# Attention and two expert layers on one core: token chunks in reversed order with split openings, and exponentials per stack with a bias and a second result

## The chip, the cores and the metric

The kernel runs on one core of a Trainium2 chip. The metric is the device time of one execution in microseconds (us), the median of several executions. The engines are named as the profile names them: PE is TensorE (matrix products), PEld its weight loads, DVE is VectorE, ACT is ScalarE, POOL is GpSimd, SP is SyncE, whose queue issues the transfers. L846 is line 846 of the kernel before; the changed kernel's numbers are a few higher and are given where they are used.

## The reference

Three stages follow one another, in float32 (w_in and w_out come as float64):

```python
# 2 batches, 8 heads, 576 positions, head width 64; q and k are drawn 8 times larger
scores = q @ k.T / sqrt(64)
mask_plain = (rel >= 0) & (rel < 32)                       # heads 0 to 3
mask_dil   = (rel >= 0) & (rel < 128) & (rel % 4 == 0)     # heads 4 to 7
scores = where(mask, scores, -1e9);  scores -= max(scores)
attn = exp(scores);  attn /= sum(attn) + 1e-9
x = (attn @ v) as 1152 tokens x 512

p = domain_probs / (sum(domain_probs) + 1e-9)              # 4 experts
x = sum over e of p[:, e] * (relu(x @ w1[e]) @ w2[e])      # hidden width 1024 each

h = x @ w_in                                               # hidden width 2048
out = (h - tanh(h)) @ w_out
```

## The kernel before

**Tokens and slices.** The 1152 tokens are cut in two sets: g = 0 holds tokens 0 to 511 (four chunks of 128; a half is 256), g = 1 holds 512 to 1151 (five chunks; a half is 320). The hidden layers are cut in 12 slices of 512 columns: 0 to 7 are the four experts', two each, and 8 to 11 belong to the second layer (w_in, w_out). A hidden slice of a set lies in four tiles f = 0 to 3 of 128 hidden columns, each as a rounded high part and a low rest, and each in two halves of the set's tokens.

The places in the program are counted by n = 0 to 13. At n = 0 and 1 (EARLY) set 0 alone goes through slices 0 and 1, in plain products of 256 columns (`whole`, L742). At n = 2 to 7 both sets go through slices 2 to 7. At n = 8 and 9 set 1 catches up on slices 0 and 1. At n = 10 (N2) to 13 (LAST) both sets go through the second layer.

**Two kinds of step on PE.** An "h" step makes a product: from n = 2 on the hidden layer is made with seven block products instead of eight (Winograd's scheme). ORDER takes products 1, 5, 6, 2, 3, 7, 4, each for t = 0 and 1, so a set has 14 such steps of six matmuls (L803). Products 2 and 3 complete halves 0 and 1 of tile f = t; products 7 and 4 complete half 1 and half 0 of tile f = t + 2. The sums that this needs run on DVE and POOL (L720, L128), then `hidden` follows. For experts that is `relu`: ACT writes the high part (L723), DVE the low one (L726), which is also what frees the PSUM bank. In the second layer it is a tanh (L774), a subtraction on DVE, and for one half a copy on ACT (L790) and a subtraction on DVE (L128).

A "y" step is one chunk of 128 tokens: 12 matmuls of 128x512 (four tiles f, three high/low passes each, L846) that accumulate in one bank. Then DVE adds the bank to the running sum `acc` (L867, L876); a sum's first addition is an ACT copy instead (L865, L871). After the experts `x2_step` transposes `acc` on PE (L892), and the second layer's input is prepared from that.

**What sets the order.** A list `steps` is written out by the rules of L926 to L940: `hs` and `ys` give a set's product and chunk steps, and `merge(a, b, at)` puts the chunks b between the products a at the places `at`. All else (sums, relus, weight splits on ACT L165 and POOL L128, attention for set 1, decoding) is handed to `later` or `when` with a due time on a planned clock that advances by `duration` of each step. `need(key)` makes everything that carries that key be written ahead of the step. Each engine executes its rows in the order written. In the kernel before, a chunk needs `("h", g)`: all pending work of that set's whole hidden slice. The slices n > 2 are merged: chunks of one set lie between the products of the other.

**Attention** has 16 head-chunks, eight for set 0 in the first 35 us (`first_attention`), eight of five stacks for set 1 during the early slices. A head-chunk holds 4 or 5 stacks of 96 keys for 128 queries. Its stages are scores (PE), `largest` (DVE L496 scale and mask, DVE L502 the negated maximum per stack, POOL L503 adds it), `exps` (ACT L510, one instruction over all stacks), `norm` (DVE L515 sums per stack, L516 and L517 add and invert, POOL L519 scales), transposes (PE L529, ACT L536) and values (PE L569).

**Decoding.** w_in and w_out are float64. DVE takes their bits apart (L672, L676, L684, L689, with ACT L683 between), 32 blocks of 128x512. Their due times are spread over a stretch [a, b) of a place n by `a + (b - a) * i / m`.

## Time and profile before

| | |
|---|---|
| median of 3 executions | 698.28 us (696.35 to 699.21) |
| the profiled execution: its time, its span | 698.15 us, 696.4 us |
| mean granted PE clock | 0.97 |
| PE busy | 641.1 us of the span (92%) |
| DVE, POOL, ACT busy | 452.2 us (65%), 381.9 us (55%), 291.7 us (42%) |
| chain of work that ended last | PE 52%, DVE 24%, POOL 8%, issue 7%, DMA 4%, ACT 4% |

Busy shares are means over the whole program. The places where PE waits are single, and few; they are read one by one from its timeline. The granted clock is a share of 2.4 GHz; the other level in this profile is 0.5, 1.2 GHz, so a clock below 1 over a stretch tells how much of the stretch ran at half speed.

### The profile page before, as it was taken

Reading aid. Unit: us, or ns where it says so; the run is one execution under the profiler, and the core shown is the slowest. Engines: PE = TensorE matmul, PEld = TensorE weight load, DVE = VectorE, ACT = ScalarE, POOL = GpSimd, SP = SyncE. Lnnn points to the kernel's source line nnn. Section 1 sums busy time; section 2 is a strip of 40 time slices with the busy share of each in tenths; the row PEclk is TensorE's granted clock in tenths of the full one; section 3 lists DMA queues with packets and bytes.
Section 4 is the critical chain, followed back from the end, with each engine's and each line's share of the span. In section 5 each row is a group of like instructions: output and inputs, shape, how many; then the busy total and the mean of one; then the engine's idle time right before and its main releaser. Section 6 shows DMA issues by size and latency. Waiting matters only on the chain.

```text
span 696.4 us, 10915 instructions
## 1 busy us (share of the span) xinstructions
PE 641.1 (92%) x4095; PEld 553.9 (80%) x4095; DVE 452.2 (65%) x859; ACT 291.7 (42%) x656; POOL 381.9 (55%) x352
## 2 busy tenths in 40 slices
PE   7876999999999999999999897999899968998997
PEld 3575878798888988978888787888698857986995
...
PEclk9998999999999999999999999899999997998999
...
GB/s 322 305 192 58 62 81 102 1 1 107 92 105 107 91 114 143 47 160 98 53 191 60 95 147 1 181 77 98 54 1 71 82 91 106 122 76 76 1 46 91
DMA packets 36693, 68.06 MB, mean 98 GB/s; under 512 B 4128, under 2 KB 10400, under 8 KB 36640
## 3 DMA queue, kind: packets, MB, share of 16 engines
...
## 4 chain that ended last, share of the span: by engine, by line
PE 52%; DVE 24%; POOL 8%; issue 7%; DMA 4%; ACT 4%; SPq 0%; DVEq 0%; POOLq 0%; ACTq 0%
PE bank_f L846 21%; PE bank_f L803 12%; PE bank_s L846 8%; POOL w L128 4%; DVE h L726 3%; PE bank_a L846 3%; PE bank_s L803 3%; DVE single L689 3%; DVE single L676 2%; DVE single L684 2%; DVE single L672 2%; DMA double<-in_moe_w_out_dram 2%; DVE bank_f L720 2%; DMA in<-single 2%; PE bank_a L803 2%
## 5 line engine op out<-in xcount | busy, mean ns | idle before, releaser
L846 PE MATMUL bank_f<-w,h 128*128 128x512 f32 x876 | 223.2, 403 | 16.9 <-ACT h L790 8.0
L846 PEld LDWEIGHTS bank_f<-w,h 128*128 128x128 f32 x876 | 163.6, 193 | 56.4 <-ACT h L790 11.1
L128 POOL TENSOR_TENSOR w<-raw,w 128x512 fp32r<-128x512 f32 x110 | 145.2, 1326 | 108.3 <-ACT w L165 105.1
L803 PE MATMUL bank_f<-x,w 128*128 128x320 f32 (+1 forms) x1218 | 180.2, 300 | 4.4 <-DVE h L726 4.4
L803 PEld LDWEIGHTS bank_f<-x,w 128*128 128x128 f32 x1218 | 172.5, 191 | 10.2 <-DVE h L726 5.4
L720 POOL TENSOR_TENSOR sums<-u,p 128x320 f32<-128x320 f32 (+1 forms) x44 | 39.4, 899 | 97.0 <-DVE u L720 97.0
L846 PE MATMUL bank_s<-w,h 128*128 128x512 f32 x312 | 80.5, 408 | 5.6 <-ACT h L723 4.5
L165 ACT ACTIVATE w<-raw 128x512 fp32r<-128x512 f32 x112 | 68.7, 627 | 30.5 <-POOL raw L128 11.6
L846 PEld LDWEIGHTS bank_s<-w,h 128*128 128x128 f32 x312 | 60.0, 197 | 20.0 <-ACT h L723 5.4
L803 PE MATMUL bank_s<-x,w 128*128 128x320 f32 (+1 forms) x402 | 61.5, 298 | 1.5 <-DVE h L726 1.5
L803 PEld LDWEIGHTS bank_s<-x,w 128*128 128x128 f32 x402 | 57.2, 190 | 4.1 <-DVE h L726 2.2
L128 POOL TENSOR_TENSOR w<-sum,w 128x512 fp32r<-128x512 f32 x36 | 49.4, 1373 | 19.0 <-ACT w L165 19.0
L867 DVE SCALAR_TENSOR_TENSOR acc<-bank_f,pn,acc 128x512 f32<-128x512 f32 x43 | 32.1, 747 | 40.3 <-PE bank_f L846 40.0
L723 ACT ACTIVATE h<-bank_f 128x320 fp32r<-128x320 f32 (+2 forms) x83 | 35.0, 430 | 41.4 <-DVE bank_f L720 40.7
L726 DVE SCALAR_TENSOR_TENSOR h<-bank_f,h 128x320 fp32r<-128x320 f32 (+2 forms) x83 | 38.9, 474 | 13.7 <-ACT h L723 12.7
L683 ACT ACTIVATE double<-double 128x512 f32<-128x512 f32 x32 | 21.6, 676 | 56.7 <-DVE single L676 51.4
L676 DVE SCALAR_TENSOR_TENSOR single<-double,single 128x512 int32<-128x512 int32 x32 | 40.6, 1269 | 1.1
L815 ACT ACTIVATE p<-bank_f 128x320 f32<-128x320 f32 (+1 forms) x60 | 23.5, 418 | 37.7 <-PE bank_f L803 37.7
L165 ACT ACTIVATE w<-sum 128x512 fp32r<-128x512 f32 x36 | 22.7, 630 | 39.3 <-POOL sum L615 21.3
L689 DVE SCALAR_TENSOR_TENSOR single<-double,single 128x512 f32<-128x512 f32 x32 | 33.3, 1042 | 8.6 <-ACT double L683 7.9
L803 PE MATMUL bank_a<-x,w 128*128 128x320 f32 (+1 forms) x228 | 37.0, 298 | 1.0 <-DVE h L726 1.0
L803 PEld LDWEIGHTS bank_a<-x,w 128*128 128x128 f32 x228 | 33.3, 190 | 2.3 <-DVE h L726 1.3
...
## 6 DMA issues: line engine op xcount, KB each, us to landing
...
```

The lines of the kernel that those rows point to most:

```text
L128: engine.tensor_tensor(out=out, in0=a, in1=b, op=ALU.subtract)
L165: nc.scalar.activation(out=hi, in_=src, func=ACTF.Copy)
L676: nc.vector.scalar_tensor_tensor(out=t, in0=high, scalar=-0x40000000, in1=t, op0=ALU.bitwise_and, op1=ALU.bitwise_or)
L683: nc.scalar.activation(out=mag, in_=mag, func=ACTF.Square)
L689: nc.vector.scalar_tensor_tensor(out=w, in0=mag, scalar=HIGH_MIN * HIGH_MIN, in1=w, op0=ALU.is_ge, op1=ALU.mult)
L720: e.tensor_tensor(out=o, in0=x, in1=y, op=ALU.add)
L723: nc.scalar.activation(out=hi, in_=src, func=ACTF.Relu)
L726: nc.vector.scalar_tensor_tensor(out=lo, in0=src, scalar=0.0, in1=hi.bitcast(F32), op0=ALU.max, op1=ALU.subtract)
L803: nc.tensor.matmul(out=b, lhsT=w[:, wi, kk, t * 128:(t + 1) * 128], rhs=x[:, kk, xi, :], start=(kk == 0 and i == 0), stop=(kk == 1 and i = ...
L815: nc.scalar.activation(out=pt[P], in_=b, func=ACTF.Copy)
L846: nc.tensor.matmul(out=y, lhsT=a, rhs=b_, start=(f == 0 and m == 0), stop=(f == NF - 1 and m == 2),)
L867: nc.vector.scalar_tensor_tensor(out=t, in0=y, scalar=p, in1=t, op0=ALU.mult, op1=ALU.add)
```

## The change

Four things change.

1. **Exponentials.** `largest` no longer has POOL add the negated maximum. `exps` issues one ACT instruction per stack of 96 keys (4 or 5 a head-chunk), with the negated maximum as its bias and the sum of its results as a second output. `norm` no longer sums on DVE.
2. **Chunks.** The chunks of a set run from the last tokens to the first (`c = last - i`). What a chunk waits for is told by tile and half instead of by set.
3. **Split openings.** `direct` cuts the first two chunks of a set in "ya" (the first tiles: three at n = 0 and 1, else two) and "yb" (the rest). It is used where the chunks follow their own set's products: n = 0 and 1, n = 2 set 0, n = 8, and n = 10 set 0. From n = 2 on the first "ya" stands ahead of the set's last product.
4. **Due times.** In the second layer the decoding's stretch goes from [a + 8, b) to [a + 4, b - 8). Set 1's attention starts 6 us later with 10.5 instead of 11 us from pair to pair. Some merge places are one earlier.

```diff
+MAKES = {
+    1: lambda t: (), 5: lambda t: (), 6: lambda t: (), 2: lambda t: (t, 0), 3: lambda t: (t, 1),
+    7: lambda t: (t + 2, 1), 4: lambda t: (t + 2, 0),
 }
...
-            nm = st.tile([128, 5], F32, tag="nm", name="nm")
-            s, r, spread = self.by_stack(t[:, 0], nm)
+            nm = self.nm[a] = st.tile([128, 5], F32, tag="nm", name="nm")
+            s, r, _ = self.by_stack(t[:, 0], nm)
             nc.vector.tensor_reduce(out=r, in_=s, axis=AX.X, op=ALU.max, negate=True)
-            later(0.5 * self.lag, lambda: nc.gpsimd.tensor_tensor(
-                out=s, in0=s, in1=spread, op=ALU.add
-            ))
 
         def exps(self, a):
-            n = self.n * BK
-            t = self.t[a]
-            nc.scalar.activation(out=t[:, 1, :n], in_=t[:, 0, :n], func=ACTF.Exp)
+            t, nm = self.t[a], self.nm[a]
+            sm = self.sm[a] = st.tile([128, 5], F32, tag="sm", name="sm")
+            for j in range(self.n):
+                ks = slice(j * BK, (j + 1) * BK)
+                nc.scalar.activation(
+                    out=t[:, 1, ks], in_=t[:, 0, ks], func=ACTF.Exp, bias=nm[:, j:j + 1],
+                    accum_out=sm[:, j:j + 1],
+                )
 
         def norm(self, a):
-            sm = st.tile([128, 5], F32, tag="sm", name="sm")
+            sm = self.sm[a]
             p, r, _ = self.by_stack(self.t[a][:, 1], sm)
-            nc.vector.tensor_reduce(out=r, in_=p, axis=AX.X, op=ALU.add)
             nc.vector.tensor_tensor(out=r, in0=r, in1=eps[:, :self.n], op=ALU.add)
...
-        key = ("h", g)
+        key = ("h", g, f, half)
...
-        later(0.0, lambda: sums_of(n, g, P, t, b, done), ("h", g))
+        later(0.0, lambda: sums_of(n, g, P, t, b, done), ("h", g, *MAKES[P](t)))
...
-            later(0.5, lambda: add(u5, u, p5, nc.gpsimd), ("h", g, t, "u5"))
+            later(0.5, lambda: add(u5, u, p5, nc.gpsimd), ("u5", g, t))
...
-    def y_step(n, g, c):
-
-        need(("h", g), ("w2", n))
-        y, done = f_bank()
-        fs = range(NF)
+    def y_step(kind, n, g, i):
+
+
+
+        c = SETS[g][1] // 128 - 1 - i
+        first = 3 if n < EARLY else 2
+        fs = {"y": range(NF), "ya": range(first), "yb": range(first, NF)}[kind]
+        if n < EARLY:
+            need(*[("h", g, f) for f in fs])
+        else:
+            halves = {c * 128 // QH[g], (c * 128 + 127) // QH[g]}
+            need(*[("h", g, f, half) for f in fs for half in halves])
+        need(("w2", n))
+        y, done = opened.pop((g, c)) if kind == "yb" else f_bank()
+        if kind == "ya":
+            opened[g, c] = y, done
...
-    FIRST, LATE, THEN = (1, 2, 3, 4, 5), (4, 5, 6, 7, 8), (5, 7, 10, 13)
+    def direct(h, n, g):
+
+        cs = ys(n, g)
+        (a0, b0), (a1, b1) = [[(kind, *step[1:]) for kind in ("ya", "yb")] for step in cs[:2]]
+        if n < EARLY:
+            return h + [a0, a1, b0, b1] + cs[2:]
+        return h[:-1] + [a0] + h[-1:] + [a1, b0, b1] + cs[2:]
+
+    FIRST, LATE, THEN = (1, 2, 3, 4, 5), (3, 4, 5, 6, 8), (5, 7, 10, 13)
     steps = []
     for n in range(EARLY):
-        steps += hs(n, 0) + ys(n, 0)
-    steps += hs(EARLY, 0) + ys(EARLY, 0) + hs(EARLY, 1)
+        steps += direct(hs(n, 0), n, 0)
+    steps += direct(hs(EARLY, 0), EARLY, 0) + hs(EARLY, 1)
...
     for n in range(NS1, N2 - 1):
-        steps += hs(n, 1) + ys(n, 1)
-    steps += hs(N2 - 1, 1) + merge(hs(N2, 0), ys(N2 - 1, 1), LATE) + ys(N2, 0) + hs(N2, 1)
+        steps += direct(hs(n, 1), n, 1)
+    steps += hs(N2 - 1, 1) + direct(merge(hs(N2, 0), ys(N2 - 1, 1), LATE), N2, 0) + hs(N2, 1)
     for n in range(N2 + 1, LAST + 1):
-        first = FIRST if n > N2 + 1 else LATE
+        first = (2, 3, 4, 5, 6) if n > N2 + 1 else LATE
...
         if n > N2:
-            a += 8.0
+            a, b = a + 4.0, b - 8.0
...
-    BEAT = 11.0
+    BEAT = 10.5
     for n in range(4):
         pair = Pair(kinds[1, n < 2], n % 2, {"s": "s", "t": "a", "x": "a"})
-        due = 3.0 + BEAT * n
+        due = 9.0 + BEAT * n
...
-        when(BEAT * 3 + 20.0 + 4.0 * c, lambda c=c: prep(1, c, True, nc.vector, nc.gpsimd), ("x", 1, False))
+        when(BEAT * 3 + 25.0 + 3.0 * c, lambda c=c: prep(1, c, True, nc.vector, nc.gpsimd), ("x", 1, False))
```

The change moves instructions as well as adding them. First place: DVE at n = 0, while the four hidden tiles of slice 0 get their low parts (`h0_702` and `h0_750` are tiles 1 and 2, `xf` and `x0` the preparation of set 0's input, `w2` a weight split, `sm` and `att` set 1's attention). Before:

```order
L128 TENSOR_TENSOR w2_703<-raw_603,w2_703 128x512
L128 TENSOR_TENSOR x0_712<-xf_383,x0_712 128x256
L128 TENSOR_TENSOR xf_383<-xf_383 128x256
L726 SCALAR_TENSOR_TENSOR h0_702<-bank_f_645,h0_702 128x512
L128 TENSOR_TENSOR xf_383<-xf_383 128x256
L128 TENSOR_TENSOR x0_751<-xf_383,x0_751 128x256
L515 TENSOR_REDUCE sm_756<-att_686 128x5
L516 TENSOR_TENSOR sm_756<-sm_756,eps_104 128x5
L517 RECIPROCAL sm_756<-sm_756 128x5
L128 TENSOR_TENSOR x0_712<-xf_383,x0_712 128x256
L128 TENSOR_TENSOR xf_383<-xf_383 128x256
L726 SCALAR_TENSOR_TENSOR h0_750<-bank_f_717,h0_750 128x512
```

After, from the same weight split:

```order
L133 TENSOR_TENSOR w2_685<-raw_611,w2_685 128x512
L133 TENSOR_TENSOR x0_689<-xf_390,x0_689 128x256
L133 TENSOR_TENSOR xf_390<-xf_390 128x256
L732 SCALAR_TENSOR_TENSOR h0_684<-bank_f_653,h0_684 128x512
L133 TENSOR_TENSOR xf_390<-xf_390 128x256
L133 TENSOR_TENSOR x0_726<-xf_390,x0_726 128x256
L133 TENSOR_TENSOR x0_689<-xf_390,x0_689 128x256
L133 TENSOR_TENSOR xf_390<-xf_390 128x256
L732 SCALAR_TENSOR_TENSOR h0_725<-bank_f_694,h0_725 128x512
L501 SCALAR_TENSOR_TENSOR att_786<-bank_s_746,mask_1_True_102 128x480
L507 TENSOR_REDUCE nm_788<-att_786 128x5
```

From this split on tile 2's low part (L726, now L732) is no longer behind the attention's sums (L515 to L517). Two scale-and-mask rows with their maxima (L496, L502), which before stand just ahead of this piece, now stand behind it (L501, L507).

Second place: PE at n = 8, where set 1's last products of slice 0 meet its own chunks (`h8_0_1` is tile 0 of set 1; `w2` and `w1` are weights, `x1` operands made from set 1's input). Before:

```order
L803 MATMUL bank_f_4579<-x1_1585,w1_4294 128x320 x6
L803 MATMUL bank_f_4591<-x1_1585,w1_4294 128x320 x6
L846 MATMUL bank_s_4607<-w2_4441,h8_0_1_4515 128x512 x3
L846 MATMUL bank_s_4607<-w2_4462,h8_1_1_4528 128x512 x3
L846 MATMUL bank_s_4607<-w2_4477,h8_2_1_4516 128x512 x3
L846 MATMUL bank_s_4607<-w2_4501,h8_3_1_4529 128x512 x3
L846 MATMUL bank_s_4625<-w2_4441,h8_0_1_4515 128x512 x3
L846 MATMUL bank_s_4625<-w2_4462,h8_1_1_4528 128x512 x3
L846 MATMUL bank_s_4625<-w2_4477,h8_2_1_4516 128x512 x3
```

After:

```order
L810 MATMUL bank_f_4603<-x1_1642,w1_4331 128x320 x6
L866 MATMUL bank_f_4615<-w2_4465,h8_0_1_4539 128x512 x3
L866 MATMUL bank_f_4615<-w2_4486,h8_1_1_4552 128x512 x3
L810 MATMUL bank_s_4625<-x1_1642,w1_4331 128x320 x6
L866 MATMUL bank_s_4636<-w2_4465,h8_0_1_4539 128x512 x3
L866 MATMUL bank_s_4636<-w2_4486,h8_1_1_4552 128x512 x3
L866 MATMUL bank_f_4615<-w2_4501,h8_2_1_4540 128x512 x3
L866 MATMUL bank_f_4615<-w2_4525,h8_3_1_4553 128x512 x3
L866 MATMUL bank_s_4636<-w2_4501,h8_2_1_4540 128x512 x3
L866 MATMUL bank_s_4636<-w2_4525,h8_3_1_4553 128x512 x3
```

The first chunk's tiles 0 and 1 now stand ahead of the last product, and tiles 2 and 3 of the first two chunks behind the openings of both.

Third place: DVE at the end of n = 11, set 1, the sums after products 7 and 4 (`u`, `sums`; `h11_2_1` is tile 2 of set 1), chunk additions (`acc`), and decoding (`single`, `double`). Before:

```order
L720 TENSOR_TENSOR bank_a_5939<-bank_a_5939,u_5781 128x320
L128 TENSOR_TENSOR x0_1440<-bank_s_5929,x0_1440 128x320
L128 TENSOR_TENSOR bank_a_5939<-bank_a_5939,sums_1439 128x320
L672 TENSOR_SCALAR single_5971<-double_5906 128x512
L676 SCALAR_TENSOR_TENSOR single_5971<-double_5906,single_5971 128x512
L876 TENSOR_TENSOR acc_5195<-bank_f_5950,acc_5195 128x512
L684 SCALAR_TENSOR_TENSOR single_5971<-double_5906,single_5971 128x512
L128 TENSOR_TENSOR h11_2_1_5829<-bank_a_5939,h11_2_1_5829 128x320
L720 TENSOR_TENSOR bank_f_5978<-bank_f_5978,u_5815 128x320
L689 SCALAR_TENSOR_TENSOR single_5971<-double_5906,single_5971 128x512
L128 TENSOR_TENSOR bank_f_5978<-bank_f_5978,sums_1439 128x320
L128 TENSOR_TENSOR h11_3_1_5860<-bank_f_5978,h11_3_1_5860 128x320
```

After:

```order
L726 TENSOR_TENSOR bank_a_5970<-bank_a_5970,u_5814 128x320
L133 TENSOR_TENSOR x0_1448<-bank_s_5960,x0_1448 128x320
L133 TENSOR_TENSOR bank_a_5970<-bank_a_5970,sums_1447 128x320
L897 TENSOR_TENSOR acc_5227<-bank_f_5981,acc_5227 128x512
L133 TENSOR_TENSOR h11_2_1_5860<-bank_a_5970,h11_2_1_5860 128x320
L726 TENSOR_TENSOR bank_f_6006<-bank_f_6006,u_5844 128x320
L133 TENSOR_TENSOR bank_f_6006<-bank_f_6006,sums_1447 128x320
L133 TENSOR_TENSOR h11_3_1_5893<-bank_f_6006,h11_3_1_5893 128x320
L897 TENSOR_TENSOR acc_5523<-bank_f_6037,acc_5523 128x512
```

The four decoding rows (L672, L676, L684, L689) that stood between the sums and the hidden tiles 2 and 3 are gone from here; the chunk addition follows the sums directly.

## Rows read from the trace of the kernel before

**Rows 1.** Page, parts 1 and 2: busy times, and PE's granted clock in tenths, 40 slices.

```profile
PE 641.1 (92%) x4095; PEld 553.9 (80%) x4095; DVE 452.2 (65%) x859; ACT 291.7 (42%) x656; POOL 381.9 (55%) x352
...
PEclk9998999999999999999999999899999997998999
```

**Rows 2.** PE's waits: line waited for and releaser: us in total, times, longest.

```profile
PE bank_a L529 <- POOL att L519: 9.1, 2, 8.1
...
PE bank_f L803 <- DVE h L726: 4.4, 4, 1.3
```

**Rows 3.** Five windows: PE, PEld, DVE, ACT, POOL busy (count), PEclk, DMA share, GB/s.

```profile
40.00:60.00 20.00, 11.87 (x114) 11.01 (x114) 18.20 (x34) 8.48 (x19) 11.40 (x15) 0.83 0.29 104
...
390.00:410.00 20.00, 17.69 (x83) 14.39 (x82) 12.81 (x22) 6.72 (x17) 6.21 (x6) 0.91 0.47 171
...
420.00:440.00 20.00, 16.17 (x77) 14.01 (x76) 12.45 (x25) 6.63 (x16) 16.28 (x13) 0.83 0.02 3
...
560.00:580.00 20.00, 11.92 (x57) 9.61 (x56) 15.80 (x28) 8.17 (x19) 10.79 (x10) 0.80 0.29 83
...
620.00:640.00 20.00, 16.97 (x75) 13.75 (x74) 11.78 (x21) 6.68 (x16) 9.42 (x8) 0.83 0.22 72
```

**Rows 4.** PE's timeline: start, us, work [idle before <- releaser].

```profile
57.08 1.09 PE L529 MATMUL bank_a<-ident,att 128*96 128x128 f32 x4 [8.13 <-POOL att L519]
...
122.22 2.23 PE L846 MATMUL bank_f<-w,h 128*128 128x512 f32 x8 [1.10 <-DVE h L726]
...
200.00 1.03 PE L846 MATMUL bank_a<-w,h 128*128 128x512 f32 x3 [0.70 <-ACT h L723]
...
397.76 0.33 PE L892 MATMUL bank_s<-ident,acc 128*128 128x128 f32 x1 [1.91 <-DVE acc L867]
...
432.75 1.65 PE L846 MATMUL bank_s<-w,h 128*128 128x512 f32 x3 [3.83 <-ACT h L723]
...
485.31 0.77 PE L892 MATMUL bank_s<-ident,acc 128*128 128x128 f32 x5 [1.18 <-DVE sums L128]
...
493.82 1.54 PE L846 MATMUL bank_f<-w,h 128*128 128x512 f32 x4 [0.90 <-DVE h L128]
...
571.38 0.73 PE L846 MATMUL bank_f<-w,h 128*128 128x512 f32 x2 [3.35 <-ACT h L790]
...
575.20 0.79 PE L846 MATMUL bank_f<-w,h 128*128 128x512 f32 x1 [3.09 <-DVE h L128]
...
577.63 1.65 PE L846 MATMUL bank_f<-w,h 128*128 128x512 f32 x3 [1.65 <-ACT h L790]
...
631.26 1.65 PE L846 MATMUL bank_f<-w,h 128*128 128x512 f32 x3 [1.44 <-ACT h L790]
```

**Rows 5.** Timelines of DVE and ACT at two of these waits.

```profile
52.69 0.68 DVE L726 SCALAR_TENSOR_TENSOR h<-bank_f,h 128x512 fp32r<-128x512 f32 x1
...
57.23 0.68 DVE L726 SCALAR_TENSOR_TENSOR h<-bank_f,h 128x512 fp32r<-128x512 f32 x1
...
429.15 0.63 ACT L165 ACTIVATE w<-sum 128x512 fp32r<-128x512 f32 x1 [3.74 <-POOL sum L128]
```

**Rows 6.** Lines by form: busy, mean ns | idle before; attention, ACT copies, decoding.

```profile
L510 ACT ACTIVATE att<-att 128x384 f32<-128x384 f32 x8 | 4.1, 517 | 8.7 <-POOL att L503 8.6
...
L503 POOL TENSOR_TENSOR att<-att,nm 128x384 f32<-128x384 f32 x8 | 6.6, 824 | 7.0 <-DVE nm L502 6.9
...
L515 DVE TENSOR_REDUCE sm<-att 128x4 f32<-128x384 f32 x8 | 4.4, 548 | 2.7 <-ACT att L510 2.7
...
L865 ACT ACTIVATE acc<-bank_f,pn 128x512 f32<-128x512 f32 x9 | 6.1, 682 | 7.2 <-PE bank_f L846 7.2
...
L871 ACT ACTIVATE acc<-bank_f 128x512 f32<-128x512 f32 x5 | 2.9, 589 | 3.8 <-PE bank_f L846 3.8
...
L676 DVE SCALAR_TENSOR_TENSOR single<-double,single 128x512 int32<-128x512 int32 x32 | 40.6, 1269 | 1.1
```

**Rows 7.** ACT's timeline, 0 to 8 us: the smallest exponential.

```profile
2.03 0.23 ACT L1139 ACTIVATE first_exp<-zero 128x32 bf16<-128x32 bf16 x1
```

More of the change, by code (lines that the diff above doesn't have):

```diff
@@ L849, in y_step @@
                 )
[L850 removed]
+        if kind != "ya":
+            later(0.0, lambda: y_sum(n, g, c, y, done), ("y", n, g))
     def y_sum(n, g, c, y, done):
```

24 lines of the change are left out of this document (15 added, 9 removed).

## The prediction

> **What bounds the kernel now.** I read the page first: PE is busy for 641.1 of 696.4 us, DVE 65%, POOL 55%, ACT 42% [rows 1]. So PE's own work is the floor, and a change that leaves its matmuls as they are, as this one does, can win only in PE's gaps and in the stretches where its clock stands at half. The row of granted clocks reads 9 in 36 of 40 slices and 8 or 7 in four [rows 1]: the losses sit in few places. I then asked for PE's waits by releaser. The longest single wait, 8.1 us, is for POOL's scaling in the attention; a group of waits of at most 1.3 us for DVE's low part is another kind [rows 2]. Windows around the long waits show a clock of 0.83, 0.91, 0.83, 0.80 and 0.83 over 20 us each [rows 3]. With levels 1 and 0.5, a mean of 0.83 is (1 - 0.83) x 20 / 0.5 = 6.8 us at half speed, 0.91 is 3.6 us, 0.80 is 8 us. PE's timeline then gives each wait its place and releaser [rows 4]; two short timelines tell what the releaser was itself behind [rows 5]. The profiled execution took 698.15 us, 0.13 below the median of 698.28, so the sum against it needs no correction.
>
> **The change part by part.**
>
> *Slice 0 (n = 0).* PE has finished its first products at 48.95 (57.08 less the wait of 8.13) and then stands still until a transpose of set 1's attention is released [rows 4]. Tile 1's low part comes at 52.69 and tile 2's at 57.23 [rows 5]: DVE was late with both. The order shows what goes from ahead of tile 2: two L496 and two L502 rows and one chain L515 to L517. A 128x384 L515 takes 0.55 us [rows 6], these are a quarter wider: some 0.65 us for each of five, and a few tenths for the chain's two small ones, 3.6 us. Tile 2 then comes at about 53.6. PE can open two chunks with tiles 0 to 2, 18 matmuls, before tile 3. At 0.23 us each at full speed (0.43 at half) these are 4 to 8 us of work that before lay behind 57.08. Tile 3 itself is hardly earlier, since the attention's rows now stand ahead of it. I take -5.0. Bounds: 0, if tile 2 is still late for another reason (its weights, POOL), and -9.5, the wait plus 1.4 us of half clock (6.8 us at half, of which 4.0 are idle until 57.08, so 2.8 x 0.5).
>
> *n = 2.* The first own chunk waits 1.10 us for DVE's low part [rows 4]; split and reversed, it begins with a tile finished several products before. -1.0, bounds 0 and -1.1.
>
> *Reversed chunks, slices 3 to 6.* At 200.00 the first chunk of set 1 waits 0.70 us for the relu of the last product [rows 4]; with its like in slices 4 to 6 that makes four. Product 4, the last, makes half 0, and the first chunk now reads half 1, ready two products (1.7 us) earlier: 4 x 0.70 = -2.8, bounds 0 and -2.8.
>
> *Slice 7's transposes.* PE waits 1.91 us for the addition of a chunk that it has only just made [rows 4], because the first transposes stand ahead of the own chunks. Now one whole chunk (12 matmuls, 2.7 us) stands ahead and covers the wait. With the 3.6 us at half behind it [rows 3], worth 1.8, that is -3.7, bounds 0 and -3.7.
>
> *n = 8.* PE waits 3.83 us for a relu [rows 4]. ACT had this relu behind a weight split which itself waited 3.74 us for POOL [rows 5]: the weight chain is late, not the products. The split opening puts 12 matmuls there where four ran before; eight more are 8 x 0.23 = 1.8 us of cover, and about 2 us of wait stay. Of the 3.4 us that 6.8 us at half cost here [rows 3] I take 1.0 back. -2.8, bounds 0 and -7.2.
>
> *n = 10.* Waits of 1.18 and 0.90 us [rows 4]. The split opening covers most of the second, earlier merge places part of the first: -1.5, bounds 0 and -2.1.
>
> *n = 11 to 12.* Three waits, 3.35 + 3.09 + 1.65 = 8.1 us [rows 4]: the last tiles' sums on DVE stand between decoding rows, of which L676 alone takes 1.27 us [rows 6]. The order shows all four decoding rows gone from this place, and a set 0 product more ahead of the first chunk. 8 us at half [rows 3], most of it idle, cost about 1.6 more. I take -7.0, bounds -2 (the waits' third, if the chain of tanh, subtraction and copy is what is late) and -9.7.
>
> *n = 12 to 13.* 1.44 us [rows 4] and 6.8 us at half [rows 3], nearly all busy, which cost 2.7: same cause. -3.5, bounds 0 and -4.1.
>
> *Exponentials.* A head-chunk loses POOL's addition, 0.82 us, and DVE's sum, 0.55 us [rows 6]. ACT did 384 columns in 0.517 us [rows 6] and 32 in 0.23 [rows 7], a slope of 0.82 ns a column, so 96 columns are 0.28 us. ACT copies with a per-partition operand take 0.682 against 0.589 us [rows 6], so a bias may add 0.09: 0.28 to 0.37 us a row, 1.1 to 1.5 for four, +0.6 to +1.0 a head-chunk. No row has a second output on ACT; its bounds are 0 and one more smallest row, 0.23 us. That leaves 1.1 to 2.4 us for four and the chain of one head-chunk between 0.8 us shorter and 0.5 longer. Eight head-chunks follow one another in the first 35 us, over four engines; only what ends the last of them counts in full. I take -1.0 for the whole, bounds -3 and +4 (eight times 0.5). For set 1, five rows in a row hold up ACT's relus by at most 3 us, which the PSUM banks in turn cover; if that cover is gone, it is a wait as at 200.00.
>
> On such rows the Trainium skill, ScalarE: Activation LUTs, section What ACT_TABLE_LOAD costs, states 280 ns + 0.833 ns a column with a pointer as bias, and about 93 ns of overlap from one to the next. By it four rows would take, as an estimate, 4 x 0.36 - 3 x 0.09 = 1.16 us, and the term would be as taken. It has no price for the second output.
>
> What goes on as before: the waits of 1.0 to 1.3 us for the low part of L726 once a slice [rows 2], since decoding in slices 3 to 7 keeps its times.
>
> *Sum:* 5.0 + 1.0 + 2.8 + 3.7 + 2.8 + 1.5 + 7.0 + 3.5 + 1.0 = 28.3, so 698.15 - 28.3 = 669.9: **670 us**.
>
> **The rivals.**
>
> *(a) Other chains end the waits.* POOL, ACT and DVE are late with weights and decoding, and PE's splitting only moves the wait by a few matmuls. For it: the ACT row behind POOL at n = 8 [rows 5]. Decoding that is moved earlier also lands beside POOL's splits; L676 takes 1.27 us on the mean [rows 6], and what slows it slows POOL as well. Then slice 0 gives 2, n = 8 gives 1, n = 11 gives 3, n = 12 gives 1.5, the reversal and the transposes 6.5: 14, so 684 us. Against it: at slice 0 and n = 11 the DVE rows named are in the order, and are gone. (The Trainium skill, SBUF — State Buffer, section SBUF: two separate sides, states that a DVE row with two SBUF inputs and a POOL row that reads SBUF lock each other out. The trace agrees as far as L676, two such inputs, takes 1.27 us on the mean [rows 6] against 0.68 for L726 with one of its inputs in PSUM [rows 5]; it does not show who held it up.)
>
> *(b) All of it is given back*, with the clock: the sum of the far bounds, 9.5 + 1.1 + 2.8 + 3.7 + 7.2 + 2.1 + 9.7 + 4.1 + 3 = 43, so 655 us. For it: each clock drop follows a wait. Against: at n = 8 the weight chain stays.
>
> *(c) Set 1's preparation is late.* Its attention begins 6 us later, its last preparation is due at 59.5 instead of 57, and PE reaches it earlier by what slice 0 gives. By the planned durations (2 x (8 x 1.44 + 4 x 2.73) for n = 0 and 1, 14 x 0.72 + 4 x 2.73 for n = 2) set 1's first product stands at 65.9. The cover of 8.9 falls to 6.4, and by 5 more in truth. A wait of up to 6 us at that product: 676 us. Against: the attention also costs less DVE and POOL.
>
> *(d) Slower: ACT becomes the bound.* If a row with a second output costs 1.3 us or more, ACT, busy 8.48 us of 20 at slice 0 [rows 3], gets 32 x 1.3 - 4.1 = 37 us more in the first 35 and 40 x 1.3 less some 5 = 47 in the next 85. The first attention ends some 20 us later and relus wait behind exponentials for 10 more: that is the point where the gains of 28 are gone, about 700 us or above. Against: the smallest row takes 0.23 us [rows 7], so it would need five times that.
>
> *(e) The change doesn't do what it says*: tiles are waited for as a whole, or in the order of an engine's latest row, so finer keys and splits release nothing, and only decoding and reversal count, 7.0 and 2.8: 688 us. Against: the orders differ at the three places.
>
> **How the numbers follow.** The forecast has 0.50; (a) 0.18; (b) 0.15; (c) 0.08; (d) 0.04; (e) 0.05. The predicted time is the forecast's, 670. 652 to 688 holds the forecast, (a), (c) and most of (b), leaving out (d), half of (e) and a third of (b): about 0.88 by these cases, less with costs that I don't know of. About 0.5%, 3.5 us, is what a measurement of this kernel can tell from no change. Faster by over that 0.92. The other 0.08 are (d) and what of (a) and (e) may come out worse than priced: within it 0.04, slower 0.04.
>
> **What would show it.** Slice 0: PE busy with chunk rows between 50 and 57 us, tile 2's low part near 53.6. Slices 3 to 6: no wait at the first chunk. Transposes: a whole chunk ahead, no wait. n = 8: a wait of about 2 us, ended by ACT behind a weight split. n = 11: at most 1 us in all, and full clock. Exponentials: rows of 0.28 to 0.6 us. PE's busy time should fall by the half clock's 8 or 9 us and its idle time by about 20. It is wrong if exponentials take 1 us, or if long waits stand in the same places behind L165 or a decoding row.

## The result, and the profile after

The changed kernel takes 675.5 us, the median of four executions (674.65 to 680.58), against 698.36 us for the kernel before, measured beside it: a ratio of 0.969 (95% interval 0.965 to 0.974). The forecast was 670 us, the range 652 to 688, the sum of the gains 28.3 us; 22.9 us came.

The profiled execution is the longest of the four: 680.58 us, a span of 678.8. Its mean granted clock is 0.980, against 0.986 to 0.992 in the other three. PE ran at half speed from 27.4 to 37.6 us in it, and the first attention took 36.04 us, against 32.44 to 33.34 in experiments 1, 2, 10, 11 and 12, which have the same code there: about 3 of the 5 us to the median lie in this place. Where the rest lies is not shown, since the other three have no trace. The page's first part and its row of granted clocks, after:

```profile
PE 638.0 (94%) x4095; PEld 554.6 (82%) x4095; DVE 437.8 (65%) x843; ACT 307.0 (45%) x784; POOL 367.3 (54%) x336
...
PEclk9888999999999999999999998979899999999999
```

Against [rows 1] PE is busy 3 us less and the span is 17.6 us shorter, so most of the gain is idle time (14.5 us). The prediction looked for 8 or 9 us less of busy time and about 20 of idle time: both fall short. PE's waits by releaser, after:

```profile
PE bank_f L866 <- ACT h L729: 3.9, 2, 2.8
...
PE bank_f L866 <- DVE h L732: 2.9, 3, 2.1
...
PE bank_s L866 <- POOL w L133: 2.1, 1, 2.1
...
PE bank_f L866 <- POOL w L133: 2.0, 1, 2.0
...
PE bank_a L810 <- DVE h L133: 2.4, 1, 2.4
```

The wait of 8.1 us for POOL's scaling that led [rows 2] is no longer there; its two of the first attention stay (2.6 and 2.8 us). What else there is now is short, and POOL's weight rows (`w`), which ended no long wait before, end two of 2 us. Where they stand shows in PE's timeline, after (start, us, work, [idle before <- releaser]):

```profile
52.98 0.73 PE L866 MATMUL bank_f<-w,h 128*128 128x512 f32 x2 [1.08 <-ACT h L729]
...
415.28 1.02 PE L866 MATMUL bank_f<-w,h 128*128 128x512 f32 x3 [2.80 <-ACT h L729]
...
448.52 0.74 PE L810 MATMUL bank_f<-x,w 128*128 128x256 f32 x4 [1.04 <-POOL w L133]
...
451.39 5.49 PE L866 MATMUL bank_f<-w,h 128*128 128x512 f32 x12 [2.12 <-DVE h L732]
...
475.09 0.77 PE L913 MATMUL bank_s<-ident,acc 128*128 128x128 f32 x5 [1.18 <-DVE sums L133]
...
484.43 0.94 PE L866 MATMUL bank_f<-w,h 128*128 128x512 f32 x2 [1.95 <-POOL w L133]
...
533.63 0.98 PE L810 MATMUL bank_a<-x,w 128*128 128x256 f32 x6 [2.37 <-DVE h L133]
...
543.72 0.73 PE L866 MATMUL bank_s<-w,h 128*128 128x512 f32 x2 [2.09 <-POOL w L133]
...
569.10 0.50 PE L866 MATMUL bank_f<-w,h 128*128 128x512 f32 x1 [1.09 <-POOL h L133]
```

Against [rows 4]: slice 0's 8.13 us are now 1.08 and less; slices 3 to 6, the transposes at slice 7 and n = 13 have no row here, their waits are gone; n = 8 keeps 2.80 of 3.83; n = 12 keeps 1.09 and smaller ones of 8.1. Of the two waits that the term of n = 10 was for, the first stands as it was (475.09, 1.18 us), and where the second stood (0.90 us for DVE) set 0's first chunk now waits 1.95 for a weight split of POOL (484.43). New are also 448.52 and 451.39 at n = 10, and 533.63 and 543.72 at n = 11.

The sum can be held against the trace place by place. PE's rows are the same work in both kernels, so the start of the first product of a set at a place n marks the same point. From one such start to the next, in us, by PE's timelines of the two profiled executions:

| from, to | before | after | difference | the sum's term |
|---|---|---|---|---|
| start to the first plain product (attention of set 0) | 35.05 | 36.04 | +1.0 | -1.0 |
| n = 0 and 1 | 72.75 | 64.76 | -8.0 | -5.0 |
| n = 2, set 0 | 26.83 | 27.12 | +0.3 | -1.0 |
| n = 2, set 1, to n = 7, set 0 | 235.53 | 231.30 | -4.2 | -2.8 |
| n = 7, set 1, and slice 7's chunks | 44.90 | 40.97 | -3.9 | -3.7 |
| n = 8 | 32.97 | 30.68 | -2.3 | -2.8 |
| n = 9 | 12.31 | 13.80 | +1.5 | 0 |
| n = 10, set 0 | 44.51 | 51.05 | +6.5 | -1.5 |
| n = 10, set 1 | 12.31 | 12.31 | 0 | 0 |
| n = 11 | 48.60 | 53.61 | +5.0 | 0 |
| n = 12 | 58.97 | 52.46 | -6.5 | -7.0 |
| n = 13, set 0 | 30.26 | 23.83 | -6.4 | -3.5 |
| the rest | 41.37 | 40.86 | -0.5 | 0 |

The differences add up to -17.6, the two spans'. Of the nine terms six came within 0.5 us or were exceeded; those of n = 2, of n = 10 and of the exponentials did not come. 13 us were lost at n = 9 to 11, where no loss had been expected. A single place carries an uncertainty of 1 to 2 us: experiment 3, which changes nothing behind the attention, takes 31.73 us at n = 8 and 46.69 at n = 10, set 0, where the kernel before takes 32.97 and 44.51.

At n = 10, set 0, the larger part of the loss is the clock. The window of this place before and after (PE, PEld, DVE, ACT, POOL busy, clock, DMA share, GB/s):

```profile
460.34:504.85 44.51, 39.21 (x215) 32.43 (x213) 23.88 (x50) 22.44 (x57) 27.57 (x26) 1.00 0.22 71
```

```profile
444.68:495.73 51.05, 43.58 (x213) 36.06 (x213) 26.93 (x56) 22.46 (x58) 30.55 (x29) 0.90 0.13 42
```

PE is idle 2.2 us longer (5.30, 7.47) and busy 4.4 us longer with the same rows; a clock of 0.90 is 10.2 us at half speed, where before there were none.

### The profile page after: what moved, and what is told of

The parts are those of the page before. It is cut to its first block, busy times and chain, and to the rows that moved or that the text cites. A ratio compares the mean times of both kernels' runs of the same rounds, so it can differ in the third digit from the quotient of the medians.

```text
span 678.8 us, 11017 instructions
## 1 busy us (share of the span) xinstructions
PE 638.0 (94%) x4095; PEld 554.6 (82%) x4095; DVE 437.8 (65%) x843; ACT 307.0 (45%) x784; POOL 367.3 (54%) x336
## 4 chain that ended last, share of the span: by engine, by line
PE 66%; DVE 12%; POOL 7%; issue 6%; ACT 5%; DMA 3%; SPq 0%; DVEq 0%; POOLq 0%; ACTq 0%
PE bank_f L866 26%; PE bank_f L810 16%; PE bank_s L866 9%; PE bank_s L810 5%; POOL w L133 3%; PE bank_a L866 3%; PE bank_a L810 3%; DMA in<-single 2%; DVE single L695 2%; ACT att L514 2%; DVE h L732 2%; PE bank_a L575 1%; DVE single L690 1%; DMA out<-single 1%; DVE u L726 1%
## 5 line engine op out<-in xcount | busy, mean ns | idle before, releaser
L866 PE MATMUL bank_f<-w,h 128*128 128x512 f32 x888 | 224.1, 401 | 10.9 <-ACT h L729 3.9
L866 PEld LDWEIGHTS bank_f<-w,h 128*128 128x128 f32 x888 | 166.0, 192 | 47.8 <-ACT h L729 4.6
L810 PE MATMUL bank_f<-x,w 128*128 128x256 f32 (+1 forms) x1212 | 180.4, 300 | 7.6 <-DVE h L732 4.7
L726 POOL TENSOR_TENSOR sums<-u,p 128x320 f32<-128x320 f32 (+1 forms) x44 | 39.5, 901 | 84.9 <-DVE u L726 84.9
L170 ACT ACTIVATE w<-raw 128x512 fp32r<-128x512 f32 x112 | 69.1, 627 | 32.8 <-PE bank_f L866 20.4
L866 PE MATMUL bank_s<-w,h 128*128 128x512 f32 x300 | 74.3, 397 | 2.5 <-POOL w L133 2.1
L866 PEld LDWEIGHTS bank_s<-w,h 128*128 128x128 f32 x300 | 55.9, 191 | 14.3 <-POOL w L133 2.5
L810 PE MATMUL bank_s<-x,w 128*128 128x320 f32 (+1 forms) x408 | 63.2, 300 | 2.8 <-DVE h L732 1.5
L689 ACT ACTIVATE double<-double 128x512 f32<-128x512 f32 x32 | 21.7, 678 | 71.2 <-DVE single L682 65.8
L732 DVE SCALAR_TENSOR_TENSOR h<-bank_f,h 128x320 fp32r<-128x320 f32 (+2 forms) x82 | 38.4, 474 | 20.4 <-ACT h L729 19.4
L170 ACT ACTIVATE w<-sum 128x512 fp32r<-128x512 f32 x36 | 22.7, 630 | 35.5 <-POOL sum L621 19.6
L810 PEld LDWEIGHTS bank_a<-x,w 128*128 128x128 f32 x228 | 33.3, 189 | 4.9 <-DVE h L133 2.6
L695 DVE SCALAR_TENSOR_TENSOR single<-double,single 128x512 f32<-128x512 f32 x32 | 31.9, 997 | 8.2 <-ACT double L689 7.4
```

Source lines behind the costliest of these rows:

```text
L170: nc.scalar.activation(out=hi, in_=src, func=ACTF.Copy)
L689: nc.scalar.activation(out=mag, in_=mag, func=ACTF.Square)
L695: nc.vector.scalar_tensor_tensor(out=w, in0=mag, scalar=HIGH_MIN * HIGH_MIN, in1=w, op0=ALU.is_ge, op1=ALU.mult)
L726: e.tensor_tensor(out=o, in0=x, in1=y, op=ALU.add)
L732: nc.vector.scalar_tensor_tensor(out=lo, in0=src, scalar=0.0, in1=hi.bitcast(F32), op0=ALU.max, op1=ALU.subtract)
L810: nc.tensor.matmul(out=b, lhsT=w[:, wi, kk, t * 128:(t + 1) * 128], rhs=x[:, kk, xi, :], start=(kk == 0 and i == 0), stop=(kk == 1 and i = ...
```

## The experiments

The kernel before ran beside each group: it took 698.9 us beside experiments 1, 2, 3 and 7, 701.6 beside 4, 10, 11 and 12, and 699.1 beside the others. So ratios are compared; the changed kernel's is 0.969 (0.965 to 0.974). Places are those of the table above, read from each kernel's profiled execution.

**1. Merge places back.**

```diff
-    FIRST, LATE, THEN = (1, 2, 3, 4, 5), (3, 4, 5, 6, 8), (5, 7, 10, 13)
+    FIRST, LATE, THEN = (1, 2, 3, 4, 5), (4, 5, 6, 7, 8), (5, 7, 10, 13)
```

> The changed kernel with the merge places LATE alone set back to (4, 5, 6, 7, 8); they hold at n = 10 and n = 11. Theory 1 (the place): the new wait of 2.12 us at 451.39 for the low part at the start of n = 10, and the 2.9 us that the half clock behind it cost, come from putting set 1's first chunk one product earlier than the relu it needs. Set back, both go: 675.5 - 5 = 670.5 us. Theory 2 (the weight chain: ACT's relu behind a weight split that waits for POOL): PE stands still for the same time wherever the chunk is put: 675.5 within 1.5 us.

Measured: 680.0 us, ratio 0.973 (0.968 to 0.977), not to be told from the changed kernel. Theory 1 falls: the waits of 1.05 and 2.13 us stand there as before, and n = 9 and 10 (set 0) take 65.9 us together, against 64.9 in the changed kernel. The place of the chunk doesn't matter; something that both wait for is late.

**2. Decoding's due times back.**

```diff
-            a, b = a + 4.0, b - 8.0
+            a += 8.0
```

> The changed kernel with the decoding's stretch alone set back to [a + 8, b). Theory 1 (decoding ended the waits at n = 11 to 12 and 12 to 13, as the prediction had it): they come back, 8.1 + 3 us with half clock, less 5 us that the waits at 533.63 (2.37 us) and 543.72 (2.09 us) give back, which earlier decoding caused: 675.5 + 6 = 681 to 683 us. Theory 2 (reversed chunks and half-wise waiting ended them): the waits stay away and those at 533.63 and 543.72 go too: 671 us.

Measured: 672.36 us, ratio 0.961 (0.957 to 0.965). Theory 2: with decoding where it was, n = 12 takes 50.73 us, still 8.2 less than before, and n = 11 takes 49.63 instead of 53.61. So earlier decoding did not end the waits at n = 12 and 13. It made the wait of 2.37 us at n = 11, which is gone here, and part of the other one there: this kernel still waits 1.19 us for POOL's weight split where the changed one waits 2.09 (543.72). DVE's timeline of the changed kernel shows how:

```profile
530.82 0.43 DVE L678 TENSOR_SCALAR single<-double 128x512 int32<-128x512 int32 x1 [5.43 <-DMA out<-single]
...
533.16 0.41 DVE L133 TENSOR_TENSOR h<-bank_a,h 128x256 fp32r<-128x256 f32 x1
```

The moved decoding row L678 waits 5.43 us for a transfer of the last block's result, and behind it on DVE stand the sums and the low part (533.16) on which PE waits 2.37 us for its bank at 533.63. The window of n = 10, set 1, and n = 11, set 0, in the kernel with the due times back (PE, PEld, DVE, ACT, POOL busy, clock, DMA share, GB/s) has PE busy throughout:

```profile
492.53:528.63 36.10, 36.10 (x230) 33.62 (x229) 20.48 (x46) 21.47 (x50) 24.53 (x24) 1.00 0.15 46
```

**3. Exponentials alone**, in the kernel before (the hunks on `largest`, `exps` and `norm`, nothing else).

> The kernel before with the exponentials alone changed. ACT's rows take 0.36 us from start to start with the row that reads the second output behind each, so four take 1.5 instead of 0.5 us, while POOL's 0.82 and DVE's 0.55 us go. Theory 1 (prediction: the chain of a head-chunk is a little shorter and the rows gone from DVE and POOL help at slice 0): 698.3 - 3 = 695 us, half of it at slice 0. Theory 2 (ACT's train delays relus and the first attention): 698 to 701 us.

Measured: 697.79 us, ratio 0.997 (0.9947 to 0.9992). Less than theory 1's 3 us, more than none: by places 0.4 us in the first attention, 1.0 at n = 0 and 1 and 1.2 at n = 8, against which its profiled execution loses 2.2 at n = 10, set 0, and 1.0 at n = 11.

**4. Exponentials back**, in the changed kernel (the same hunks, reversed).

> The changed kernel with the exponentials as before (POOL adds, one ACT row, DVE sums). Theory 1 (the change alone gave 0.3%, a little): 675.5 + 1 to 2 = 677 us. Theory 2 (with the attention later the rows it takes from DVE and POOL stand at slice 0 no more, and ACT's train only costs): 673 to 675 us.

Measured: 675.95 us, ratio 0.965 (0.962 to 0.969): not to be told from the changed kernel. By places both theories are half right. In the first attention PE waits for POOL's scaling at some 11 us: 2.62 us here and 2.47 before (2.54 to 3.07 in experiments 7, 8 and 9); with the new exponentials 1.30 to 2.14 in experiments 1, 2, 3, 5, 10, 11 and 12, but 2.60 in the changed kernel's profiled execution. Where PE ran at half speed behind it (from 11 to 13 us on), the first attention takes 35.05 to 35.34 us with the old (before, experiments 4, 7 and 8) and 34.62 and 34.75 with the new ones (experiments 3 and 5); where it did not, the new ones take 32.4 to 33.3 us (experiments 1, 2, 10, 11, 12) and the old ones 33.73 (experiment 9). So they win 0.3 to 1.3 us there, and more where the clock stays up in the one and not in the other, which differs between kernels with the same code for this part. Against that, n = 2, set 0, takes 25.24 us here and 27.12 in the changed kernel: ACT's train costs 1.9, together with the attention's later due times, for with the earlier ones the new exponentials take 25.48 there (experiment 11).

**5. New exponentials for set 0, old ones for set 1**, on the kernel of experiment 10. `exps` returns after one row over all stacks where `self.lag` is 1, and POOL's addition and DVE's sum are there for set 1 alone.

> On the kernel without decoding at n = 8 and 9 (661.6 us): set 0's exponentials stay per stack with bias and second output, set 1's go back to one ACT row with POOL's addition and DVE's sum. Theory 1 (per stack shortens the first attention by 2 us, since four engines take turns there, and costs 2 us behind ACT's train of ten rows during n = 1 and 2): 661.6 - 2 = 659.6 us. Theory 2 (the 2 us are PE's attention work that only changes places): 661.6 within 0.7 us.

Measured: 659.74 us (659.32 to 660.32), ratio 0.944 (0.942 to 0.946), against 661.61 and 0.945 (0.941 to 0.949) of experiment 10: no difference that stands clear of the intervals. At n = 2, set 0, theory 1 holds: 25.24 us against 27.10. But the profiled execution took 34.75 us for the first attention, whose code is the same in both, against 32.51; PE ran at half speed from 12.0 to 15.5 us in it and not in the other. Whether the mixture is worth 2 us stays open.

**6. Bias, but no second output.** `accum_out` goes, DVE's sum comes back.

> The changed kernel with the exponentials per stack and bias, but without the second output; DVE sums again. One look for the price of the second output: in the changed kernel a row of 96 columns starts 0.36 us after the last, with a row of 0.19 us between that reads the sum. Theory 1 (the reading row costs about 0.09 us of the 0.36): rows start every 0.27 us. Theory 2 (it is hidden behind the next row): every 0.36 us. The first attention is at least 1 us longer than in the changed kernel, since DVE's 0.55 us a head-chunk are back; 675.5 + 1 = 676 to 678 us.

Measured (one execution): 672.8 us. The time says nothing against 675.5 from a single run; the price is in ACT's timeline. The changed kernel, then this one:

```profile
8.42 0.38 ACT L514 ACTIVATE att<-att,nm 128x96 f32<-128x96 f32 x1 [6.16 <-DVE nm L507]
...
8.70 0.18 ACT L514 ACTIVATION_READ_ACCUMULATOR att<-att,nm 128x1 f32 x1
...
8.79 0.36 ACT L514 ACTIVATE att<-att,nm 128x96 f32<-128x96 f32 x1
```

```profile
12.36 1.16 ACT L514 ACTIVATE att<-att,nm 128x96 f32<-128x96 f32 x4
```

With the second output each row is followed by one that reads the sum, and rows start 0.36 us apart (8.42, 8.79). Without it four rows take 1.16 us together, one of 0.36 and three more at 0.27 apart. Theory 1: the second output costs 0.09 us a row, not the 0.19 of its own. At n = 2, set 0, this kernel takes 26.20 us, between the 27.12 with the second output and the 25.24 of one row for all stacks: there ACT's time counts.

**7. Chunks reversed and waiting by half, alone**, in the kernel before: `c = SETS[g][1] // 128 - 1 - i`, the finer keys, and `direct` returning `h + ys(n, g)`; exponentials, due times and merge places as before.

> The kernel before with reversed chunks and waiting by tile and half alone: no split openings, old exponentials, due times and merge places. Theory 1 (terms of the prediction): slices 3 to 6 give 4 x 1.05 us as in the changed kernel's trace, the transposes of slice 7 some 2.9 us, the second layer at most 2: 698.3 - 8 = 690 us. Theory 2 (reversal also ends the waits at n = 11 to 13, since the first chunk no longer needs product 4): 698.3 - 18 = 680 us.

Measured: 685.46 us, ratio 0.980 (0.976 to 0.983). Between the theories in time. By places theory 2: n = 12 is 5.2 us shorter, n = 13, set 0, 4.7, without any change to decoding. What keeps the total from 680 is n = 10, set 0: 53.21 us, 8.7 longer than before.

**8. Finer waiting alone**: experiment 7 with `c = i`.

> The kernel before with waiting by tile and half alone: chunks still from the first tokens to the last. Theory 1 (what counts is which half the first chunk reads; product 4, the last, makes half 0, which the first chunk still needs): nothing in slices 3 to 6, little elsewhere: 698.3 - 1 = 697 us. Theory 2 (the finer keys let the rows that a chunk doesn't need be written behind it, and this alone ends the waits at n = 11 to 13): 698.3 - 9 = 689 us.

Measured: 698.7 us, ratio 0.9993 (0.9974 to 1.0011). Theory 1; finer keys alone are worth nothing.

**9. Reversal alone**: experiment 7 with `halves = {0, 1}`.

> The kernel before with reversed chunks alone: every chunk makes all rows of its set's hidden slice be written ahead of it, as before. Theory 1 (an engine's row waits only for what it reads, so the order of halves is enough): 685.5 us as with both, within 2. Theory 2 (rows for product 4 written ahead on DVE and ACT hold up the sums of the chunks and of the next set): 690 us or more.

Measured: 684.71 us, ratio 0.979 (0.977 to 0.982), as with both. Theory 1 by the time. But the places differ: with whole keys slice 7's transposes still wait for the addition of a chunk,

```profile
392.13 0.70 PE L912 MATMUL bank_s<-ident,acc 128*128 128x128 f32 x4 [2.61 <-DVE acc L887]
```

and n = 7, set 1, takes 45.23 us, as before, against 40.95 in experiment 7; n = 10, set 0, takes 47.30 against 53.21. So the equal times hide a gain of the finer keys at slice 7 and a loss behind it. PE's timeline of this kernel where the three waits of n = 12 stood:

```profile
562.38 1.32 PE L865 MATMUL bank_f<-w,h 128*128 128x512 f32 x5
...
564.66 0.50 PE L865 MATMUL bank_f<-w,h 128*128 128x512 f32 x1 [0.97 <-POOL h L133]
...
565.77 0.73 PE L865 MATMUL bank_f<-w,h 128*128 128x512 f32 x2 [0.61 <-ACT h L170]
...
569.08 0.80 PE L865 MATMUL bank_f<-w,h 128*128 128x512 f32 x1 [0.70 <-POOL h L133]
```

Of 3.35 + 3.09 + 1.65 us there remain 0.97, 0.61 and 0.70, with decoding's due times and keys as in the kernel before. Before, the waits were ended by a copy on ACT (L790) and a subtraction on DVE, which belong to half 0; the ones that remain are ended by POOL and by a rounding on ACT (L170), which make half 1.

**10. No decoding at n = 8 and 9**, on the kernel of experiment 2.

```diff
-    for n, m in [(n, 4) for n in range(EARLY + 1, NS1)] + [(N2 + 1, 5), (N2 + 2, 4)]:
+    for n, m in [(n, 4 + (n > 4)) for n in range(EARLY + 1, NS1)] + [(N2 + 1, 5), (N2 + 2, 4)]:
...
-        if n == NS1 - 1:
-            where += [start["y", NS1, 1, 0] - 4.0 + 4.0 * i for i in range(3)]
```

> On the kernel with decoding's dues set back (672.4 us): the three blocks that were decoded during n = 8 and 9 are spread over n = 5 to 7 (five instead of four each). Theory 1 (at n = 9 ACT's weight splits for n = 10 stand behind a decoding row that waits for DVE; POOL's chain and the relus behind it come late, and PE waits 1.05 + 2.13 us and runs 6.8 us at half): these go, 672.4 - 6 = 666 us, with up to 1 us given back at n = 5 to 7. Theory 2 (the chain of weights is late by itself): 671 to 673 us.

Measured: 661.61 us, ratio 0.945 (0.941 to 0.949). Theory 1, and more than it said: n = 9 falls from 13.71 to 12.31 us and n = 10, set 0, from 50.99 to 44.55, what they took before; n = 2 to 7 lose another 3.1, where the waits of 1.06 us for L732 at n = 5 and 6 are gone. This is the best of all kernels but for experiment 5, which can't be told from it. How a decoding block holds PE up shows from the end of the chain backwards. ACT of the changed kernel:

```profile
431.35 0.68 ACT L689 ACTIVATE double<-double 128x512 f32<-128x512 f32 x1 [7.75 <-DVE single L682]
...
431.92 0.62 ACT L170 ACTIVATE w<-raw 128x512 fp32r<-128x512 f32 x1
...
449.86 0.63 ACT L170 ACTIVATE w<-sum 128x512 fp32r<-128x512 f32 x1 [3.67 <-POOL sum L133]
...
450.39 0.75 ACT L729 ACTIVATE h<-bank_f 128x320 fp32r<-128x320 f32 x2
```

The relu at 450.39, which PE waits for by way of DVE's low part at 451.39, stands behind a weight split that waited 3.67 us for POOL; POOL's chain began late: the split at 431.92 stands behind the decoding's L689, which waited 7.75 us for DVE, and the next split, at 436.85, behind another L689 that waited 3.73. The wait of the weight split for POOL is as long in experiment 10 (3.75 us at 436.35); what differs is when POOL's chain begins. Its sum L621, in the changed kernel and in experiment 10:

```profile
441.81 1.29 POOL L621 TENSOR_TENSOR sum<-raw 128x512 f32<-128x512 f32 x1
```

```profile
428.20 1.30 POOL L621 TENSOR_TENSOR sum<-raw 128x512 f32<-128x512 f32 x1
```

That is 10.9 us behind PE's start of n = 9 in the changed kernel (430.88) and 5.6 in experiment 10 (422.63). In the kernel before (PE at 448.02) it is 6.2, in experiments 9 and 7 (440.14 and 436.02) 8.3 and 8.4: with the block in place the chain falls further behind as PE comes earlier. Experiment 12 doesn't fit in, with 8.3 us at 430.75 and yet 53.14 us at n = 10, set 0; so this distance is not all that counts. DVE and SP's queue (issues, and what SP waited for: us, times, longest, 400 to 440 us):

```profile
430.16 0.43 DVE L678 TENSOR_SCALAR single<-double 128x512 int32<-128x512 int32 x1 [4.63 <-issue]
```

```profile
425.55 0.33 SPq L668 DMA_DIRECT2D double<-in_moe_w_out_dram  x1
...
426.45 0.99 SPq L610 DMA_DIRECT2D raw<-in_moe_w_dram  x2
...
427.54 6.78 SPq L610 DMA_DIRECT2D raw<-in  x2
```

```profile
SPq L668 <- DVE single L695: 28.8, 1, 28.8
```

The block's load (L668) sat 28.8 us at the head of SP's queue for a buffer that an earlier block (L695) still held; DVE began the block (L678) 4.6 us after it was issued. The weight loads `raw` for n = 9 and 10 stood behind it; all were issued together at 425 to 434 us. Without the block at this place the same loads are issued earlier, against PE's arrival at n = 9 at 422.63 in this kernel and 430.88 in the changed one, and PE meets one wait of 0.62 us there:

```profile
397.11 7.06 SPq L610 DMA_DIRECT2D raw<-in_moe_w_dram  x2
...
416.76 1.63 SPq L610 DMA_DIRECT2D raw<-in  x2
```

```profile
437.89 3.02 PE L866 MATMUL bank_f<-w,h 128*128 128x512 f32 x12 [0.62 <-DVE h L732]
```

The kernel before has the same wait at SP and issues these loads at 439.67:

```profile
SPq L662 <- DVE single L689: 31.3, 1, 31.3
```

```profile
439.67 1.01 SPq L604 DMA_DIRECT2D raw<-in_moe_w_dram  x2
```

That is 13.2 us later than the changed kernel; but its PE came to n = 9 17.1 us later. By the 3.9 us between, PE got ahead of its loads. The experiment takes away the late loads and ACT's decoding rows together; which of the two costs more is not separated. Nor is every loss at n = 10 the block's: the waits of 1.18 and 1.95 us that the changed kernel has at 475.09 and 484.43 stand in experiment 10 too:

```profile
458.80 0.77 PE L913 MATMUL bank_s<-ident,acc 128*128 128x128 f32 x5 [1.18 <-DVE sums L133]
...
468.12 1.05 PE L866 MATMUL bank_f<-w,h 128*128 128x512 f32 x2 [1.95 <-POOL w L133]
```

**11. Attention's due times back.**

```diff
-    BEAT = 10.5
+    BEAT = 11.0
...
-        due = 9.0 + BEAT * n
+        due = 3.0 + BEAT * n
...
-        when(BEAT * 3 + 25.0 + 3.0 * c, lambda c=c: prep(1, c, True, nc.vector, nc.gpsimd), ("x", 1, False))
+        when(BEAT * 3 + 20.0 + 4.0 * c, lambda c=c: prep(1, c, True, nc.vector, nc.gpsimd), ("x", 1, False))
```

> The changed kernel with the due times of set 1's attention and preparation alone set back (BEAT 11, from 3, preparation as before). Theory 1 (the 6 us of shift clear DVE at the end of the first attention and at slice 0): first plain product 2.5 us later, slice 0 some 4 us longer: 675.5 + 6 = 681 to 682 us. Theory 2 (the split openings and the missing rows of the exponentials do it, the shift only moves rows): within 1.5 us of 675.5.

Measured: 682.49 us, ratio 0.975 (0.971 to 0.979), by the ratios some 4 us more, with intervals that overlap; the places decide. Theory 1 for the place: n = 0 and 1 take 69.97 us, 5.2 more than in the changed kernel; n = 2, set 0, takes 25.48, 1.6 less. The first attention is not longer (33.34 us), so that part of theory 1 falls.

**12. No split openings.** `direct` returns `h + ys(n, g)`.

> The changed kernel without the split openings: direct returns h + ys(n, g), chunks stay reversed. Theory 1 (prediction: 18 matmuls of cover at n = 0 and 8 at n = 8): slice 0 loses 4 us, n = 1 some 1, n = 8 some 2, n = 10 up to 1: 675.5 + 7 = 682 to 683 us. Theory 2 (the low parts come early enough without, since DVE's rows are gone): within 2 us of 675.5.

Measured: 683.13 us, ratio 0.975 (0.972 to 0.979), by the ratios some 4 us more, with intervals that just overlap. Theory 1, but half as large: n = 0 and 1 take 67.75 us, 3.0 more, n = 9 and 10 (set 0) together 0.6 more, n = 8 no more at all (30.28).

## Why the prediction was right, and where it was not

**Slice 0.** Right in the main, and 3 us larger. The low part of tile 2 was to come at 53.6 us, and DVE's timeline of the changed kernel has

```profile
50.66 0.68 DVE L732 SCALAR_TENSOR_TENSOR h<-bank_f,h 128x512 fp32r<-128x512 f32 x1
...
53.45 0.68 DVE L732 SCALAR_TENSOR_TENSOR h<-bank_f,h 128x512 fp32r<-128x512 f32 x1
...
57.32 0.68 DVE L732 SCALAR_TENSOR_TENSOR h<-bank_f,h 128x512 fp32r<-128x512 f32 x1
```

against 52.69 and 57.23 [rows 5] and, for tile 3, before:

```profile
59.11 0.68 DVE L726 SCALAR_TENSOR_TENSOR h<-bank_f,h 128x512 fp32r<-128x512 f32 x1
```

Since the first plain product came 1.0 us later in this execution, tile 2 gained 4.8 us against it, where 3.6 were forecast, and tile 3 gained 2.8, where hardly any was. The prediction left out one move on PE: the transposes of set 1's attention, on which PE had waited 8.13 us, stood ahead of the first chunk, and in the changed kernel they stand behind 36 chunk rows:

```profile
62.27 0.60 PE L535 MATMUL bank_a<-ident,att 128*96 128x128 f32 x4
```

With the attention's due times set back (experiment 11) PE has nine chunk rows ahead of them and waits for low and high parts:

```profile
51.17 0.49 PE L866 MATMUL bank_f<-w,h 128*128 128x512 f32 x1 [2.52 <-DVE h L732]
...
53.59 1.72 PE L866 MATMUL bank_f<-w,h 128*128 128x512 f32 x3 [1.93 <-ACT h L729]
...
55.10 1.05 PE L535 MATMUL bank_a<-ident,att 128*96 128x128 f32 x4
```

Of the 8 us the shift of attention gives 5.2 (experiment 11) and the split 3.0 (experiment 12).

**Reversed chunks, transposes, n = 8.** In slices 3 to 6 mechanism and size held: four waits of 0.70 us gave 4.2 us, 1.05 each by the table. Slice 7 gave 3.9 of 3.7, but the reversal needs the finer keys for it (experiment 9). n = 8 gave 2.3 of 2.8, with the weight chain still ending a wait of 2.80 us, and not by the mechanism given: without the split it takes no longer (30.28 us, experiment 12), and experiments 3 and 8 are 1.2 and 1.5 us shorter there with neither split nor reversal.

**n = 12 and 13.** The sizes were right (-6.5 and -6.4 for -7.0 and -3.5), the reason was not. The prediction put the waits down to the decoding rows that stood between the sums, and their removal to the new due times. Experiments 2 and 9 show that the reversal does it: the first chunk now reads the half that product 7 makes, and not product 4's, the last, whose tanh, subtraction, copy (L790) and second subtraction end the waits of [rows 4]. The prediction had this chain only as a bound at which the term would shrink to -2; it was the cause, and the reversal that took it off the path stood in the sum for slices 3 to 6 alone. That these 10.5 us of the sum came true was luck: more than one part of the change touches this place, and one that was not priced there did it. Reversal alone gives 5.5 and 4.7 us (experiment 9); which of the other parts gives the rest, the earlier merge places of n = 12 and 13 among them, was not tested, nor was earlier decoding alone in the kernel before.

**Exponentials.** A row of 96 columns was priced at 0.28 to 0.37 us with 0 to 0.23 for the second output; it took 0.36 from start to start, 0.09 of it for the second output. The term of -1.0 fits the first attention alone, 0.3 to 1.3 us and more with a clock that stays up; that ACT's train costs 1.9 at n = 2 (experiments 4 and 5) was named as a cover that might be gone, and not counted. This is also why the term of n = 2 did not come: with either the old exponentials or the old due times of the attention this place takes 25.2 to 25.5 us (experiments 4, 7 and 11), against 26.83 before and 27.12 in the changed kernel. In the kernel before, where set 1's attention lies earlier, the change alone gives 0.3% (experiment 3). The Trainium skill, ScalarE: Activation LUTs, section What ACT_TABLE_LOAD costs, states figures from which the estimate of 1.16 us for four rows came; without the second output they take 1.16 us. It has no price for the second output.

**The step that failed** is *n = 10*: "The split opening covers most of the second, earlier merge places part of the first: -1.5". The place took 6.5 us more instead (2.2 of waits, 4.4 of busy time at half speed), with 1.5 more at n = 9. The split opening is not what cost it (53.14 us without, experiment 12), and neither are the merge places (experiment 1). The prediction counted the waits that were there and not what PE's earlier arrival would meet: a decoding block whose removal gives the whole loss back (experiment 10). By the timelines its load held the loads of weights on SP's queue and its rows held ACT, so that splits, POOL's chain and the relus came late together. Even without the block the term is not there: n = 10, set 0, takes 44.55 us, as before, since the wait of 1.18 us is untouched and the first own chunk waits 1.95 us for a weight split. Rival (a) had the mechanism, but spread over places where it did not hold. Rival (c) has almost the measured time, 676 us, and is not what happened: at set 1's first product (127.92 us) PE does not wait. The second omission is n = 11, where the moved decoding was priced at nothing and cost 4.0 us (experiment 2). By the table, all places that fell short of their terms did so by 18.8 us, and those that exceeded theirs (slice 0 by 3.0, n = 13 by 2.9, slices 3 to 6 by 1.4) by 8.0: 28.3 - 18.8 + 8.0 = 17.5, the spans' difference. By the medians 5 us of the 28.3 are missing.

**Open** is the clock in the first 36 us: PE's wait of 2.81 us for POOL at about 27 us is followed by 3.4 us at half speed in experiments 1, 2 and 10, by 6.8 in 11 and 12 and by 10.2 in the changed kernel's profiled execution, with the same code for the first attention. That reversal with whole keys takes 47.30 us at n = 10, set 0, and with finer keys 53.21 is for the larger part the clock too: PE is busy 39.92 and 43.80 us there, at a mean clock of 0.96 and 0.90, and idle 7.4 and 9.4. Why the clock stays at half speed three times as long (3.4 and 10.2 us) behind waits of like size is open.
